# Two expert slots fetched as quarter rows and turned on VectorE instead of on TensorE

## The chip, the cores and the metric

The kernel runs on one core of a Trainium2 chip. The metric is device time in microseconds (us) for one execution. Three executions of the kernel before took 553.5, 553.92 and 554.93 us; their median is 553.92 us. A further execution was profiled, and took 553.22 us.

## The reference

For 8 batches of 8 heads, 576 positions and 64 dimensions, an attention through 32 memory columns, and behind it a mixture of 8 experts in which every token goes to one expert:

```
a = softmax(phi, axis=positions)                 # 32 memory columns a head
k_m, v_m = a^T k, a^T v                          # 32 x 64 a head
x = softmax(q k_m^T / 8) v_m                     # 4608 tokens x 512
e = argmax(x @ w_gate)                           # each token's expert, 8 of them
h = relu(x @ w1[e])                              # 512 -> 1024
out = softmax(x @ w_gate)[e] * sigmoid(x @ w_output_gate)[e] * (h @ w2[e])
```

All tensors are float32.

## The kernel before

The program has two overlapping parts. The attention runs for the first 110 us or so and writes its result x, with the gate factor of each token, as rows of 576 floats into the DRAM tensor `xs` (four groups of 144: 128 columns of x and 16 that hold the gate). The experts' work is a stream of *slots*. A slot is one expert and two or three blocks of 128 tokens which chose it. The tokens are not known beforehand: the kernel counts and ranks them on the chip while the attention runs (`rank`, `route_early`, `route_late`) and makes lists of row numbers with small matmuls (`table`). There are three lists: "a" serves slots 0 and 1, "b" serves slots 2, 3 and 4, and "l", which needs the whole attention, serves all later slots. In this data 14 slots run, 10 of three blocks and 4 of two.

A slot of three blocks goes through these steps. GpSimd gathers its rows from `xs` by indirect DMA into `xg` (`gather`, L538 and L532). The rows are turned so that the 512 columns of x lie on partitions, in four chunks (`turn_x`, chunk number c), and each chunk is split into a high part `xh` (a cast by ScalarE, L1091) and a low part `xl` (the rest, by VectorE, L1092). The *first half* of the slot on TensorE is 96 matmuls (L1241) that read the chunks in order 0, 1, 2, 3 for each of 8 output groups: per chunk one matmul with `xh`, one with `xl`, one with `xh` again. ScalarE (L1245) and VectorE (L1246) take their result out of PSUM. The *second half* is 72 matmuls (L1278) in 12 steps of 6; the results `y` are scaled by ScalarE (L1213) and scattered to the output by GpSimd (L1214), three DMAs a slot. The weights come as tiles `w` of 512 KB on SyncE's queue, each split into high and low part `whl` by ScalarE (L577) and VectorE (L591). After the attention has ended ten `whl` tiles are kept, so their splitting runs ahead of the matmuls.

Rows are turned in one of two ways. A *whole* slot is gathered with one DMA a block, three in all, and each chunk is turned by three TensorE transposes against the identity (L1089) into PSUM. A *quartered* slot is gathered with four DMAs a block, twelve in all, from an index list `idx_q` that puts row quarters so that VectorE's 32 x 32 block transpose (L1073) finishes the turn in SBUF. It also needs four small ScalarE copies (L1066) that gather the gate factors, and its `w` tiles are read from a copy with rows in another order. In the kernel before slots 0 to 4 are whole, and all later ones quartered.

The order of instructions on each engine is that in which the Python code emits them, and each engine works in order. While a slot's second half is emitted, `nxt(c)` emits the turn of the next slot's chunk c at steps 1, 4, 6, 9 and 10 (`TURN`). A whole slot uses the first four of these: transposes, `xh` and `xl` of chunk c together. A quartered slot uses all five: at c it emits VectorE's transpose of chunk c, and `xh` and `xl` of chunk c - 1. Behind every step `hook()` emits a few instructions of the routing that is still to be done (`route_late` up to the list "l"), which are mostly small VectorE operations between L346 and L272. `xg` has three buffers, so that a slot's gather can be emitted while the slot two before it runs.

Of the kernel before, what the change touches and what calls it, by code (L numbers as in the profile page):

```python
# [8 lines left out]
F32 = mybir.dt.float32  # L9
F32R = mybir.dt.float32r  # L10
BF16 = mybir.dt.bfloat16
I32 = mybir.dt.int32
# [5 lines left out]
P = 128  # L18
B, H, S, D, M = 8, 8, 576, 64, 32
NTOK, DM, E, F = 4608, 512, 8, 1024  # L20
# [8 lines left out]
NPS = (2, 3)  # L29
NPT, NPP, NSS = 5, 4, 22  # L30
NPE = sum(NPS)
NB3, NB2 = 3 * NPT, 2 * NPP
NBL = NB3 + NB2 + NSS
# [20 lines left out]
LATE = {"lg": 8, "w": 2, "ct": 8, "pe": 3, "dve": 2}  # L54
# [1 line left out]
PUMP = (2, 1)  # L56
TURN = {3: (1, 4, 6, 9, 10), 2: (0, 1, 2, 3, 4)}
LAST = 1
WHOLE = tuple(range(NPE))
XQ = 144  # L60
XROW = 4 * XQ

# [5 lines left out]
def attention_moe(tc, phiT, kv, qT, wgo, wall, out):  # L68
    nc = tc.nc
    V, A, G, T = nc.vector, nc.scalar, nc.gpsimd, nc.tensor  # L70

    with contextlib.ExitStack() as ctx:
        cp = ctx.enter_context(tc.tile_pool(name="cp", bufs=1))
# [4 lines left out]
        ident = cp.tile([P, P], F32, name="ident")  # L78
# [15 lines left out]
        idx = {}  # L94
        for nm, n in (("a", 3 * NPS[0]), ("b", 3 * NPS[1]), ("l", NBL)):
            idx[nm] = (cp.tile([P, n], I32, name="idx_g" + nm), cp.tile([P, n], I32, name="idx_o" + nm),
                       cp.tile([P, 4, n], I32, name="idx_q" + nm) if nm == "l" else None)
        slot = cp.tile([P, NSLOT + 1], I32, name="slot")
        ctx.enter_context(tc.manual_schedule())
        ohcs = [cp.tile([P, E], BF16, name=f"ohc{i}") for i in range(NBP)]  # L100
# [2 lines left out]
        rt = ctx.enter_context(tc.tile_pool(name="rt", bufs=1))  # L103
# [107 lines left out]
        def table(nm, q, nch, nblk):  # L211

            while nm == "l" and "rl" not in env:
                yield
            bw = (env["rl"] if nm == "l" else rt).tile([P, nch, 2, nblk], BF16, name="bw" + nm)
            w = min(nch, 9 * NBL // nblk // 9 * 9)
            for c in range(0, nch, w):
                b3 = [P, w, nblk]
                eq = rt.tile([P, 9 * NBL], BF16, name="eq")
                eq = eq[:, 0:w * nblk].rearrange("p (c b) -> p c b", c=w)  # L220
                V.tensor_tensor(eq, iota_blk[:, 0:nblk].unsqueeze(1).to_broadcast(b3),
                                q[:, c:c + w].unsqueeze(2).to_broadcast(b3), ALU.is_equal)
                yield
                for i in range(2):
                    V.tensor_tensor(bw[:, c:c + w, i], eq,
                                    tok_hl[:, i, c:c + w].unsqueeze(2).to_broadcast(b3), ALU.mult)
                yield
            yield
            yield from take_pr()
            yield from hold(LATE["pe"])  # L230
            pi = ps_r.tile([P, 2, NBL], F32, name="pr")
            for c in range(nch):
                T.matmul(pi[:, :, 0:nblk], Aw[:, c], bw[:, c], start=(c == 0), stop=(c == nch - 1))
            yield
            yield from hold(LATE["dve"])
            hl = rt.tile([P, 2, NBL], BF16, name="hl_i")
            iv = rt.tile([P, NBL], F32, name="iv")
            i2 = rt.tile([P, NBL], F32, name="i2")
            ivv, i2v, hlv = iv[:, 0:nblk], i2[:, 0:nblk], hl[:, :, 0:nblk]
            V.tensor_copy(hlv, pi[:, :, 0:nblk])  # L240
            yield
            V.scalar_tensor_tensor(ivv, hlv[:, 0], 64.0, hlv[:, 1], ALU.mult, ALU.add)
            if nm != "l":
                taken.clear()
            yield
            ig, io, iq = idx[nm]
            V.tensor_scalar(ig[:], ivv, 1.0, 0.0, ALU.subtract, ALU.max)
            V.tensor_scalar(i2v, ivv, 0.0, 100000.0, ALU.is_equal, ALU.mult)
            yield
            V.scalar_tensor_tensor(io[:], ivv, -1.0, i2v, ALU.add, ALU.add)  # L250
            if nm != "l":
                return
            for z in order:
                if z["nm"] == nm and not z["quart"]:
                    z["listed"] = True

            rep = env["rep"]
            pq = ps_r.tile([P, 4, 2, NBL], F32, name="pr")
            for b in range(4):
                T.matmul(pq[:, b, :, 0:nblk], rep[:, b], hlv, start=True, stop=True)  # L260
            yield
            yield from hold(LATE["dve"])
            t4 = env["rl"].tile([P, 4, NBL], F32, name="iq")
            t4v = t4[:, :, 0:nblk]
            V.tensor_copy(t4v, pq[:, :, 1, 0:nblk])
            yield
            V.scalar_tensor_tensor(t4v, pq[:, :, 0, 0:nblk], 64.0, t4v, ALU.mult, ALU.add)
            taken.clear()
            yield
            V.tensor_scalar(t4v, t4v, 1.0, 0.0, ALU.subtract, ALU.max)  # L270
            yield
            V.tensor_scalar(iq[:], t4v, 4.0, quad[:, 0:1], ALU.mult, ALU.add)  # L272
# [6 lines left out]
        def route_early(k):  # L279
# [48 lines left out]
            V.tensor_tensor(t1, t1, t3, ALU.mult)  # L328
            yield
            yield from table(nm, t1, nch, 3 * n)  # L330
            for z in order[s0:s0 + n]:
                z["listed"] = True
            if k == 0:
                gathers(0)
# [121 lines left out]
        env = {}  # L456
        clock = [0]

        taken = []

        def take_pr():

            while taken:
                yield
            taken.append(1)

        def hold(n):

            if "open" not in env:
                return  # L470
            end = clock[0] + n
            while clock[0] < end:
                yield

        def force():
            clock[0] += 1
            (rou if rou.gens else late if late.gens else att).step()
# [25 lines left out]
        for s in range(NSLOT):  # L503
            nb = 3 if s < NPE + NPT else 2 if s < NPE + NPT + NPP else 1
            if s < NPE:
                k = s >= NPS[0]
                nm, q0, rows = "ab"[k], 3 * (s - NPS[0] * k), (k + 2) * NCH * P
            else:
                j = s - NPE
                q0 = 3 * j if nb == 3 else NB3 + 2 * (j - NPT) if nb == 2 else NB3 + NB2 + j - NPT - NPP  # L510
                nm, rows = "l", NTOK
            slots.append({"s": s, "nb": nb, "q0": q0, "idx": idx[nm], "rows": rows,
                          "nm": nm, "quart": s not in WHOLE,
                          "known": False, "listed": False})
# [6 lines left out]
        def quarters(z, k):  # L521

            return 2 if (z["nb"], k) == (2, 1) else 4

        def gather(z):
            z["xg"] = xgs.tile()
            for k in range(z["nb"]):
                q = z["q0"] + k
                if z["quart"]:
                    rows = 4 * z["rows"]  # L530
                    for b in range(quarters(z, k)):
                        G.indirect_dma_start(  # L532
                            out=z["xg"][:, k, XQ * b:XQ * b + XQ], out_offset=None,
                            in_=xs[0:z["rows"]].rearrange("t (a q) -> (t a) q", a=4),
                            in_offset=bass.IndirectOffsetOnAxis(ap=z["idx"][2][:, b, q:q + 1], axis=0),
                            bounds_check=rows - 1, oob_is_err=False)
                    continue
                G.indirect_dma_start(  # L538
                    out=z["xg"][:, k], out_offset=None, in_=xs[0:z["rows"]],
                    in_offset=bass.IndirectOffsetOnAxis(ap=z["idx"][0][:, q:q + 1], axis=0),  # L540
                    bounds_check=z["rows"] - 1, oob_is_err=False)

        def known(*zs):
            for z in zs:
                z["known"] = True
# [64 lines left out]
        gat = [0, NPE + NPT + NPP]  # L610

        def gathers(i, must=0):

            while gat[0] < min(gat[1], i + xgs.size):
                z = order[gat[0]]
                if not z["listed"]:
                    if gat[0] >= must:
                        break
                    force()
                    continue  # L620
                gather(z)
                gat[0] += 1

        pa = ctx.enter_context(contextlib.ExitStack())
# [731 lines left out]
        def run(st):  # L1356
# [8 lines left out]
            def hook():  # L1365
                gathers(i)
                clock[0] += not att.gens
                att.step(HOOK[0])
                (rou if rou.gens else late).step(HOOK[1])

            for i in range(lo, hi):
                gathers(i, i + 1)
                if i == lo:
                    for c in range(5):
                        turn_x(order[i], c)

                def nxt(c):
                    if i + 1 < hi:
                        gathers(i, i + 2)
                        turn_x(order[i + 1], c)  # L1380

                if order[i]["nb"] > 1:
                    several(i, st, nxt, hook)
                else:
                    single(i, st, nxt)
                if "hs" not in env and (i == LAST or not att.gens):
                    settle()
# [6 lines left out]
        n = NPE + NPT + NPP  # L1394
# [52 lines left out]
```

## Time and profile before

| | |
|---|---|
| median of three executions | 553.92 us |
| the profiled execution | 553.22 us |
| its span in the trace | 551.5 us |
| TensorE matmuls busy | 507.9 us, 92% of the span |
| VectorE busy | 354.1 us, 64% |
| ScalarE busy | 288.0 us, 52% |
| GpSimd busy | 231.8 us, 42% |

Span and time of the profiled execution lie 1.7 us apart, which is launch and end. Busy shares are means over the span; matmuls are pipelined, so what a matmul costs is read from the distance of starts, not from its own duration. PE is TensorE, PEld its weight load, DVE VectorE, ACT ScalarE, POOL GpSimd, SP SyncE. Slot 0 starts at 119 us and slot 13 ends at 542 us.

### The profile page before, as it was taken

What the parts mean: (1) busy time and instruction counts of PE and PEld (TensorE: products, weight loads), DVE (VectorE), ACT (ScalarE), POOL (GpSimd) and SP (SyncE); (2) the same over time, 40 slices, a digit from 0 to 9 for tenths busy, and PEclk for the clock granted to TensorE, in tenths of its full rate; (3) what the DMA queues carried; (4) which work ended last, traced back from release to release, by engine and by line L of the source; (5) the groups of instructions that cost most, each with busy time, mean ns of one, the idle gap of its engine ahead of it and who ended that gap; (6) DMA issues with size and microseconds to landing.
All of it is one profiled execution on the core that took longest, in us unless ns stands there. A gap on an engine that the chain in (4) does not pass through costs nothing. (4 is left out here: it accounts for less than half of the span.)

```text
span 551.5 us, 10575 instructions
## 1 busy us (share of the span) xinstructions
PE 507.9 (92%) x3859; PEld 439.1 (80%) x3859; DVE 354.1 (64%) x779; ACT 288.0 (52%) x536; POOL 231.8 (42%) x254
## 2 busy tenths in 40 slices
PE   3788767689999999999999999999999999999993
PEld 2555545469789889898898989898999899888982
DVE  4376687877866659997454564954786387629310
ACT  3467465545535455553444545854785386548310
POOL 2244374860444134510467472655447363821101
PEclk9969799979999999999999999999999999999997
DMA  8999999995567756973466574876686577743001
GB/s 306 419 391 386 408 356 372 302 413 170 152 185 219 248 162 226 315 201 117 149 183 204 173 239 129 247 217 217 176 259 188 189 236 245 220 151 98 30 21 43
DMA packets 41998, 123.54 MB, mean 224 GB/s; under 512 B 10256, under 2 KB 10320, under 8 KB 41552
## 3 DMA queue, kind: packets, MB, share of 16 engines
q1 hardware_dynamic: 35136, 102.71, 56.5%
q0 software_dynamic: 6800, 20.06, 10.2%
q8 instruction: 32, 0.52, 0.4%
q14 instruction: 30, 0.25, 0.2%
HBM read 102.40 MB, written 20.35 MB: 223 GB/s over the span
## 5 line engine op out<-in xcount | busy, mean ns | idle before, releaser
L1278 PE MATMUL bps<-whl,hh 128*128 128x512 f32 x640 | 192.4, 393 | 0.0
L1241 PE MATMUL bps<-xh,whl 128*128 128x384 f32 x640 | 165.8, 336 | 0.0
L591 DVE TENSOR_TENSOR whl<-w,whl 128x1024 fp32r<-128x1024 f32 x112 | 138.2, 1239 | 10.9 <-ACT whl L577 10.8
L1278 PEld LDWEIGHTS bps<-whl,hh 128*128 128x128 f32 x640 | 119.9, 188 | 24.3 <-issue 0.2
L577 ACT CAST whl<-w 128x1024 fp32r<-128x1024 f32 x112 | 116.5, 1045 | 21.2 <-PE bps L1278 16.5
L1241 PEld LDWEIGHTS bps<-xh,whl 128*128 128x128 f32 x640 | 115.8, 188 | 1.1 <-ACT hh L1245 0.4
L532 POOL DMA_INDIRECT xg<-xs,idx_ql x84 | 97.3, 1158 | 25.6 <-issue 23.5
L1241 PE MATMUL bps<-xl,whl 128*128 128x384 f32 x320 | 107.0, 334 | 0.0
L1278 PE MATMUL bps<-whl,hl 128*128 128x512 f32 x240 | 93.7, 390 | 0.0
L1246 DVE SCALAR_TENSOR_TENSOR hl<-bps,hh 128x384 fp32r<-128x384 f32 x80 | 44.0, 554 | 60.3 <-ACT hh L1245 60.3
L1245 ACT ACTIVATE hh<-bps 128x384 fp32r<-128x384 f32 x80 | 38.9, 492 | 76.2 <-PE bps L1241 76.1
L1214 POOL DMA_INDIRECT out<-y,idx_ol x23 | 25.2, 1095 | 110.6 <-ACT y L1213 54.3
L1241 PEld LDWEIGHTS bps<-xl,whl 128*128 128x128 f32 x320 | 60.1, 188 | 0.3
L1278 PEld LDWEIGHTS bps<-whl,hl 128*128 128x128 f32 x240 | 45.1, 188 | 8.5
L1236 PE MATMUL bps<-xh,whl 128*128 128x384 f32 x128 | 37.7, 338 | 0.0
L872 POOL TENSOR_TENSOR ea<-ea,mx 128x512 f32<-128x512 f32 (+1 forms) x20 | 19.2, 960 | 43.3 <-DVE mx L870 39.0
L1237 PE MATMUL bps<-xh,whl 128*128 128x256 f32 x128 | 35.7, 279 | 0.0
L1213 ACT ACTIVATE y<-bps,gx 128x512 f32<-128x512 f32 x19 | 13.1, 687 | 40.0 <-PE bps L1278 33.4
L905 ACT COPY xo<-bpd 128x576 f32<-128x576 f32 x36 | 22.2, 641 | 21.4 <-PE bpd L903 9.7
L903 PE MATMUL bpd<-ve_b,aT 64*128 64x144 f32 (+1 forms) x320 | 28.6, 331 | 3.4 <-DVE ea L866 3.2
L1214 POOL DMA_INDIRECT out<-y,idx_ob x9 | 10.1, 1119 | 49.8 <-ACT y L1213 37.8
L988 POOL TENSOR_SCALAR Aw<-iota_row,row 128x128 bf16<-128x128 bf16 x36 | 26.0, 738 | 8.9 <-DVE row L978 8.9
(267 smaller groups left out, 588.2 us busy)
## 6 DMA issues: line engine op xcount, KB each, us to landing
w<-wall SPq DMA_DIRECT2D x112, 512.0 KB, 4.4
kvt<-kv SPq DMA_DIRECT2D x32, 512.0 KB, 8.1
xs<-xo SPq DMA_DIRECT2D x16, 576.0 KB, 7.4
qt<-qT SPq DMA_DIRECT2D x16, 512.0 KB, 8.5
ph<-phiT SPq DMA_DIRECT2D x3, 1152.0 KB, 11.7
kv<-kv SPq DMA_DIRECT2D x4, 512.0 KB, 8.5
xg<-xs,idx_ql POOLq DMA_INDIRECT x84, 4.5
ph<-phiT SPq DMA_DIRECT2D x4, 288.0 KB, 3.2
```

What stands on the lines that cost most here:

```text
L532: G.indirect_dma_start(out=z["xg"][:, k, XQ * b:XQ * b + XQ], out_offset=None, in_=xs[0:z["rows"]].rearrange("t (a q) -> (t a) q", a=4), i ...
L577: A.copy(hl[:, 0], w[:])
L591: V.tensor_tensor(hl[:, 1], w[:], hl[:, 0].bitcast(F32), ALU.subtract)
L903: T.matmul(px[to:to + n, r, sl], z["aT"][h, o:o + n], ves[2 * bp + b][h, g], start=True, stop=True)
L988: (G if AWP else V).tensor_scalar(Aw[:, bp * NCH + c], iota_row[:], row[:, c:c + 1], None, ALU.is_equal)
L1214: G.indirect_dma_start(out=out, out_offset=bass.IndirectOffsetOnAxis(ap=z["idx"][1][0:n, z["q0"] + k:z["q0"] + k + 1], axis=0), in_=y[0:n] ...
L1236: T.matmul(pb, w[:, 0, o:o + P], x[0][:, cc], start=(cc == 0), stop=False)
L1237: T.matmul(pb[:, 0:256], w[:, 1, o:o + P], x[0][:, cc, 0:256], start=False, stop=(cc == 3))
L1241: T.matmul(pb, w[:, b, o:o + P], x[a][:, cc, 0:n_], start=(n == 0), stop=(n == 11))
L1245: A.activation(h_[:, j], pb, AF.Relu)
L1246: V.scalar_tensor_tensor(l_[:, j], pb, 0.0, h_[:, j].bitcast(F32), ALU.max, ALU.subtract)
L1278: T.matmul(py[k], a, w[:, b, DM * f:DM * f + DM], start=(u == 4 and f == 0 and n == 0), stop=(u == 7 and f == 1 and n == len(ps) - 1))
```

## The change

Slots 3 and 4 become quartered. For that the list "b" also gets an index list of row quarters, `idx_qb`. The late list's is made with a tile `rep` of repeated identity slices in bfloat16, which does not exist yet when list "b" is made; list "b" uses sixteen matmuls of 128 x 32 identity slices on a float32 copy `hlf` of the list instead, into four 32-partition strips. The gather of slots 3 and 4 is emitted one DMA a hook. For all lists the quarter matmuls now first take the shared PSUM buffer (`take_pr`) and wait three hooks (`hold`), which moves those of list "l" too.

```
-WHOLE = tuple(range(NPE))
+WHOLE = (0, 1, 2)
...
-                       cp.tile([P, 4, n], I32, name="idx_q" + nm) if nm == "l" else None)
+                       cp.tile([P, 4, n], I32, name="idx_q" + nm) if nm != "a" else None)
...
+            if nm == "b":
+                hlf = rt.tile([P, 2, 3 * NPS[1]], F32, name="hlf", bufs=1)
+                A.copy(hlf[:], pi[:, :, 0:nblk])
...
-            if nm != "l":
-                taken.clear()
+            taken.clear()
...
-            if nm != "l":
+            if nm == "a":
                 return
...
-            rep = env["rep"]
+            yield from take_pr()
+            yield from hold(LATE["pe"])
             pq = ps_r.tile([P, 4, 2, NBL], F32, name="pr")
             for b in range(4):
-                T.matmul(pq[:, b, :, 0:nblk], rep[:, b], hlv, start=True, stop=True)
+                if nm == "l":
+                    T.matmul(pq[:, b, :, 0:nblk], env["rep"][:, b], hlv, start=True, stop=True)
+                else:
+                    for a in range(4):
+                        T.matmul(pq[32 * a:32 * a + 32, b, :, 0:nblk], ident[:, 32 * b:32 * b + 32], hlf[:],
+                                 start=True, stop=True)
...
-            t4 = env["rl"].tile([P, 4, NBL], F32, name="iq")
+            if nm == "l":
+                t4 = env["rl"].tile([P, 4, NBL], F32, name="iq")
+            else:
+                t4 = rt.tile([P, NSS, E], F32, name="cle")
...
                             bounds_check=rows - 1, oob_is_err=False)
+                        yield
                     continue
...
+            yield True
...
-                gather(z)
+                z.setdefault("gen", gather(z))
+                slow = z["nm"] == "b" and gat[0] >= must
+                while not next(z["gen"]):
+                    if slow:
+                        return
                 gat[0] += 1
```

Two places show how instructions move. The first is VectorE at the end of slot 2's second half, where slot 3's chunks are turned among the small operations of `route_late`. Before, from the `xl` of chunk 2 to just behind that of chunk 3:

```order
L1092 TENSOR_TENSOR xl<-bps,xh 128x384
L419 TENSOR_TENSOR cse<-cse 128x44
L421 TENSOR_TENSOR cse<-cse,kk 128x44
L423 TENSOR_TENSOR cse<-cse 128x22
L425 TENSOR_TENSOR slot<-cse 128x22
L203 TENSOR_TENSOR tm<-ohg,tb 128x288 x2
L591 TENSOR_TENSOR whl<-w,whl 128x1024
...
L430 TENSOR_TENSOR q_3276<-q_3276,jg 128x36
L431 TENSOR_TENSOR q_3279<-q_3279,jg 128x36
L1092 TENSOR_TENSOR xl<-bps,xh 128x384
L433 TENSOR_SCALAR ov<-q_3276,os 128x36
L435 TENSOR_TENSOR q_3276<-q_3276,ov 128x36
```

In the change (its line numbers are 12 to 18 higher: L1091 is the block transpose, L1110 is `xl`, L605 the low part of the weights), from the transpose of chunk 2 to the `xl` of chunk 3:

```order
L1091 STREAM_TRANSPOSE xt<-xg 128x384
L1110 TENSOR_TENSOR xl<-xt,xh 128x384
...
L203 TENSOR_TENSOR tm<-ohg,tb 128x288 x2
L605 TENSOR_TENSOR whl<-w,whl 128x1024
...
L442 TENSOR_TENSOR q_3352<-q_3352,jg 128x36
L443 TENSOR_TENSOR q_3355<-q_3355,jg 128x36
L1091 STREAM_TRANSPOSE xt<-xg 128x384
L1110 TENSOR_TENSOR xl<-xt,xh 128x384
L445 TENSOR_SCALAR ov<-q_3352,os 128x36
L447 TENSOR_TENSOR q_3352<-q_3352,ov 128x36
L1110 TENSOR_TENSOR xl<-xt,xh 128x384
L449 TENSOR_TENSOR q_3355<-q_3355,q_3352 128x36
```

The `xl` of chunk 2 now stands where that of chunk 3 stood, behind the transpose of chunk 3; the `xl` of chunk 3 stands one step later, behind two routing operations.

The second place is GpSimd from slot 1's second half on (`idx_gb` is list "b" by whole rows, `idx_qb` by quarters, `idx_ql` the late list by quarters, `out` the scatter of results). Before:

```order
L538 DMA xg<-xs,idx_gb 128x576 x6
L932 TENSOR_TENSOR w__2712<-lg,lm 128x72
L1214 DMA out<-y,idx_oa 4608x512 x3
L538 DMA xg<-xs,idx_gb 128x576 x3
L988 TENSOR_SCALAR Aw<-iota_row,row 128x128 x9
L1214 DMA out<-y,idx_ob 4608x512 x4
L532 DMA xg<-xs,idx_ql 128x144 x12
L1214 DMA out<-y,idx_ob 4608x512 x2
L532 DMA xg<-xs,idx_ql 128x144 x6
```

In the change:

```order
L551 DMA xg<-xs,idx_gb 128x576 x3
L544 DMA xg<-xs,idx_qb 128x144 x5
L950 TENSOR_TENSOR w__2743<-lg,lm 128x72
L544 DMA xg<-xs,idx_qb 128x144 x7
L1232 DMA out<-y,idx_oa 4608x512 x3
L544 DMA xg<-xs,idx_qb 128x144 x8
L1006 TENSOR_SCALAR Aw<-iota_row,row 128x128 x6
L544 DMA xg<-xs,idx_qb 128x144
L1006 TENSOR_SCALAR Aw<-iota_row,row 128x128 x3
L544 DMA xg<-xs,idx_qb 128x144 x3
L1232 DMA out<-y,idx_ob 4608x512 x6
L544 DMA xg<-xs,idx_ql 128x144 x18
```

Slots 3 and 4 take 24 gathers instead of 6, and the twelve gathers of slot 5 (the first of `idx_ql`) now stand behind all three scatters of slot 3, where they stood behind its first.

## Rows read from the trace of the kernel before

**Rows 1.** The page: busy us and share of the span by engine; and busy tenths of TensorE and VectorE in 40 slices of 13.8 us.

```profile
PE 507.9 (92%) x3859; PEld 439.1 (80%) x3859; DVE 354.1 (64%) x779; ACT 288.0 (52%) x536; POOL 231.8 (42%) x254
PE   3788767689999999999999999999999999999993
DVE  4376687877866659997454564954786387629310
```

**Rows 2.** Busy time of each engine in two stretches: the end of slot 2's first half with its second half and the start of slot 3, then most of slot 3. Behind the counts stand the granted clock, the DMA share and GB/s.

```profile
209.00:242.00 33.00, 33.00 (x173) 29.82 (x172) 32.49 (x98) 19.00 (x27) 13.43 (x13) 1.00 0.75 246
243.00:270.00 27.00, 27.00 (x168) 23.48 (x167) 19.69 (x36) 10.88 (x17) 1.11 (x2) 1.00 0.47 143
```

**Rows 3.** TensorE in order of time (start, duration): the first row of slot 2's second half, the matmul before one group of slot 3's transposes and the two starts behind it, the start of slot 3's first half and of its second, and the starts of slot 4's second half and of slot 5.

```profile
216.24 0.39 PE L1278 MATMUL bps<-whl,hh 128*128 128x512 f32 x1
...
218.77 0.39 PE L1278 MATMUL bps<-whl,hh 128*128 128x512 f32 x1
219.01 0.49 PE L1089 MATMUL bps<-ident,xg 128*128 128x128 f32 x3
219.25 0.48 PE L1278 MATMUL bps<-whl,hh 128*128 128x512 f32 x1
219.57 0.39 PE L1278 MATMUL bps<-whl,hl 128*128 128x512 f32 x1
...
234.07 0.33 PE L1241 MATMUL bps<-xh,whl 128*128 128x384 f32 x1
...
250.73 0.39 PE L1278 MATMUL bps<-whl,hh 128*128 128x512 f32 x1
...
287.12 0.39 PE L1278 MATMUL bps<-whl,hh 128*128 128x512 f32 x1
...
303.48 0.33 PE L1241 MATMUL bps<-xh,whl 128*128 128x384 f32 x1
```

**Rows 4.** TensorE in order of time during the attention: two runs of sixteen small float32 matmuls with 32 weight columns, each with the row that follows it.

```profile
16.34 0.71 PE L765 MATMUL pk<-kv,a 128*32 128x128 f32 x16
16.98 0.28 PE L771 MATMUL pk<-zero 1*128 1x256 bf16 x1
...
19.42 0.32 PE L805 MATMUL bpa<-wg,vT_b 64*32 64x16 f32 x16
19.66 0.66 PE L736 MATMUL bpa<-ident,ph 128*128 128x128 f32 x4
```

**Rows 5.** VectorE in order of time: the last row before the stretch of rows 2 with an idle time ahead of it (in brackets, with what ended it), slot 3's four `xl`, and the rows behind the fourth.

```profile
208.64 0.56 DVE L1246 SCALAR_TENSOR_TENSOR hl<-bps,hh 128x384 fp32r<-128x384 f32 x1 [1.24 <-ACT hh L1245]
...
222.07 0.55 DVE L1092 TENSOR_TENSOR xl<-bps,xh 128x384 fp32r<-128x384 f32 x1
...
226.70 0.55 DVE L1092 TENSOR_TENSOR xl<-bps,xh 128x384 fp32r<-128x384 f32 x1
...
230.50 0.55 DVE L1092 TENSOR_TENSOR xl<-bps,xh 128x384 fp32r<-128x384 f32 x1
...
234.58 0.55 DVE L1092 TENSOR_TENSOR xl<-bps,xh 128x384 fp32r<-128x384 f32 x1
235.05 0.23 DVE L433 TENSOR_SCALAR ov<-q,os 128x36 f32<-128x36 f32 x1
...
235.54 0.20 DVE L437 TENSOR_TENSOR q<-q,q 128x36 f32<-128x36 f32 x1
```

**Rows 6.** VectorE in order of time while slot 5, a quartered one, is turned: two block transposes and an `xl`, each with the row that follows it, and the `xl` of chunk 3.

```profile
289.90 0.58 DVE L1073 STREAM_TRANSPOSE xt<-xg 128x384 f32<-128x384 f32 x1 [0.36 <-DMA out<-y,idx_ob]
290.40 1.18 DVE L591 TENSOR_TENSOR whl<-w,whl 128x1024 fp32r<-128x1024 f32 x1
291.51 0.57 DVE L1073 STREAM_TRANSPOSE xt<-xg 128x384 f32<-128x384 f32 x1
292.00 0.52 DVE L1092 TENSOR_TENSOR xl<-xt,xh 128x384 fp32r<-128x384 f32 x1
292.43 1.22 DVE L591 TENSOR_TENSOR whl<-w,whl 128x1024 fp32r<-128x1024 f32 x1
...
303.49 0.56 DVE L1092 TENSOR_TENSOR xl<-xt,xh 128x384 fp32r<-128x384 f32 x1 [0.79 <-ACT xh L1091]
```

**Rows 7.** GpSimd in order of time: slot 2's third scatter, the first and last gather of slot 5, and the first gather behind slot 4's third scatter; and ScalarE's row that first needed the last of slot 5's gathers.

```profile
240.53 1.15 POOL L1214 DMA_INDIRECT out<-y,idx_ob  x1 [3.35 <-ACT whl L577]
...
269.86 1.47 POOL L532 DMA_INDIRECT xg<-xs,idx_ql  x1 [0.30 <-issue]
...
284.99 1.25 POOL L532 DMA_INDIRECT xg<-xs,idx_ql  x1 [0.30 <-issue]
...
312.54 1.04 POOL L532 DMA_INDIRECT xg<-xs,idx_ql  x1 [0.30 <-issue]
...
289.59 0.19 ACT L1066 COPY gx<-xg 32x3 f32<-32x3 f32 x1 [0.32 <-DMA xg<-xs,idx_ql]
```

**Rows 8.** Windows as in rows 2 at two pauses of TensorE during the attention and behind the first of them; and one form of matmul in order of time in the second of these windows and in the expert stage.

```profile
78.00:81.30 3.30, 0.04 (x1) 0.05 (x1) 2.25 (x6) 1.32 (x5) 3.30 (x6) 1.00 1.04 350
81.50:84.70 3.20, 3.20 (x43) 2.53 (x49) 0.82 (x4) 1.97 (x5) 1.94 (x3) 0.50 1.04 334
88.30:91.50 3.20, 1.51 (x44) 0.92 (x36) 2.99 (x12) 0.91 (x3) 1.63 (x4) 1.00 1.03 409
...
81.92 2.29 PE L903 MATMUL bpd<-ve_b,aT 64*128 64x144 f32 x16
...
170.71 1.25 PE L903 MATMUL bpd<-ve_b,aT 64*128 64x144 f32 x16
```

More of the change, by code (lines that the diff above doesn't have):

```diff
@@ L255, in table @@
                     z["listed"] = True
-            rep = env["rep"]
+            yield from take_pr()
+            yield from hold(LATE["pe"])
             pq = ps_r.tile([P, 4, 2, NBL], F32, name="pr")
             for b in range(4):
-                T.matmul(pq[:, b, :, 0:nblk], rep[:, b], hlv, start=True, stop=True)
+                if nm == "l":
[4 more added lines that the diff above has]
+                                 start=True, stop=True)
             yield
             yield from hold(LATE["dve"])
-            t4 = env["rl"].tile([P, 4, NBL], F32, name="iq")
+            if nm == "l":
+                t4 = env["rl"].tile([P, 4, NBL], F32, name="iq")
+            else:
+                t4 = rt.tile([P, NSS, E], F32, name="cle")
+                t4 = t4[:].rearrange("p a b -> p (a b)")[:, 0:4 * nblk].rearrange("p (a b) -> p a b", a=4)
             t4v = t4[:, :, 0:nblk]
```

## The prediction

> **What bounds the kernel now.** I read the page first, then windows, then TensorE and the engines that feed it in order of time. Over the span TensorE is busy 92% and VectorE 64% [rows 1]; from slice 9 on, where the slots run, TensorE stands at 9 in every slice. So the time is set by TensorE's work behind 119 us and by each pause in it. The windows show the second thing: from 209 to 242 us VectorE too is busy, 32.49 of 33.00 us, and from 243 to 270 only 19.69 of 27.00 [rows 2]. In order of time VectorE last waits for something at 208.64 us [rows 5]; behind that it works through a queue that is already there. There the routing of `route_late`, the weights that fill the ten `whl` tiles and slot 2's own results come together. The reader is to see that TensorE does not wait for this yet: slot 3 starts at 234.07 us, right behind slot 2 [rows 3], while the last thing it needs, the `xl` of its chunk 3, runs from 234.58 to 235.13 us [rows 5]. A first half of 96 matmuls takes 16.66 us (234.07 to 250.73) [rows 3], 0.174 us each, and that `xl` is read by its eleventh matmul, at 234.07 + 10 x 0.174 = 235.81. The slack is 0.7 us.
>
> **What it removes.** Slots 3 and 4 lose 24 TensorE transposes, in eight groups of three. A second half without transposes takes 303.48 - 287.12 = 16.36 us, slot 2's, with four groups, takes 234.07 - 216.24 = 17.83 [rows 3]. From 218.77 to 219.57 there are two stream matmuls (2 x 16.36 / 72 = 0.45 us) and one group, 0.35 us. Four groups are thus 1.4 to 1.47 us, and two slots give back 2.8 us.
>
> **What it adds on TensorE.** Sixteen small float32 matmuls with 32 weight columns and 18 data columns. The trace has no such form; sixteen with 16 columns and half the rows take 19.66 - 19.42 = 0.24 us, sixteen with 128 columns 16.98 - 16.34 = 0.64 us [rows 4]. I take 0.4 us. They stand in slot 1 and shift everything behind alike.
>
> **What it moves to VectorE.** Eight block transposes of 0.50 us (289.90 to 290.40) [rows 6]; in slot 4 they lie in a stretch with idle time [rows 2], and cost nothing as long as that lasts. The four index operations and ScalarE's copy `hlf` fall into slot 1, before the queue builds; the eight copies of gate factors on ScalarE, 0.2 us each [rows 7], lie beside casts. In slot 3 the transposes enter the full queue, and the order matters more than their length. Up to chunk 2's `xl` in the change, four transposes are new and one `xl` fewer stands ahead (0.43 us, 292.00 to 292.43) [rows 6]. Chunk 2's `xl` stands where chunk 3's did, so it starts at 234.58 + 4 x 0.50 - 0.43 = 236.15 and ends 0.52 later, at 236.67. TensorE ends slot 2 at 216.24 + 16.36 = 232.60 and needs that `xl` for its eighth matmul, at 233.82. It waits 2.85 us. Behind chunk 2's `xl` come two routing operations, 235.54 - 235.05 = 0.49 us [rows 5], then chunk 3's `xl`: it ends at 236.15 + 0.43 + 0.49 + 0.52 = 237.59, three matmuls after the restart would be 237.19. Another 0.4, together 3.25 us. Bounds: if the earlier transposes found gaps, only chunk 3's own would count and the wait would be 234.58 + 0.50 + 0.52 - 233.82 = 1.8 us; if ScalarE's cast of chunk 3, which stands between two VectorE operations, came last, another 0.5 us, 3.75 in all. I take 3.25, since rows 2 leave half a microsecond of gaps in 33. Who waits behind it: slot 3's results and `y` by as much; of weights ten tiles are ahead.
>
> **What it moves on GpSimd.** The gathers of slots 3 and 4 have over 20 us to spare each: twelve at about 1.4 us are 17 us and start where three started. Slot 5 is different. Its twelve gathers now follow slot 3's third scatter. Slot 2's third scatter starts 6.5 us behind its slot's end (240.53 - 234.07) and lasts 1.15, so a gather could start at +7.9; behind slot 4's it starts at +9.1 (312.54 - 303.48) [rows 3, 7]. I take +8.5 behind slot 3's end. From slot 5's first gather to the first use of its last data were 289.59 - 269.86 = 19.7 us [rows 7]: data at +28.2. From there ScalarE and VectorE need four transposes, three weight splits of 1.11 (290.40 to 291.51) between them [rows 6], four `xl` and ScalarE's first cast, about 7.7 us to chunk 3's `xl`: +35.9. TensorE, through slot 4 without transposes, needs it at 16.66 + 16.36 + 1.74 = +34.8. A wait of 1.1 us, with +7.9 one of 0.5, with +9.1 one of 1.7; with the spare of the 269.86 start none. I take 1.1.
>
> **The clock.** A pause can cost more than itself. Behind 78.00 to 81.30 us, in which TensorE did 0.04 us of work, its granted clock was 0.50, the 1.2 GHz level, for 81.50 to 84.70; behind 88.30 to 91.50, with 1.51 us of work, no fall is seen [rows 8]. At the lower level sixteen matmuls of one form took 2.29 us, at 2.4 GHz 1.25 [rows 8], so 3.2 us at the lower level lose 3.2 x (1 - 1.25 / 2.29) = 1.45 us. A pause of 3.25 us resembles the first case more. If part of the low stretch lies on the pause itself it costs less; between 0 and 1.45 I take 1.0.
>
> **The sum.** -2.8 + 0.4 + 3.25 + 1.1 + 1.0 = +2.95 us, on 553.22 us: 556.2. The profiled execution lies 0.7 us under the median and under all three timed ones, so the same sum on the median gives 556.9. I predict 556.7 us.
>
> **Two rules against the trace.** The rows give 0.12 us of TensorE's time per transpose. The Trainium skill ("VectorE: DVE Perf Modes", The three transpose paths) gives a 128 x 128 transpose 390 ns on TensorE in bfloat16 and 311 ns on VectorE, in blocks; by that figure 24 of them would be an estimated 9.4 us on TensorE, and no run here shows one alone. By the rows' starts it is a third of that. The shares of the whole span say that TensorE is the engine to relieve and VectorE the one with room [rows 1]. The Trainium skill ("Perfetto Trace Analysis", Identifying the Most-Contended Engine) says to optimize the engine with the highest occupancy, and by that alone the change would bring 2.4 us; it adds that the most contended engine can change over time, and with that rows 2 agree.
>
> **The rivals.**
> - *The gain stands* (0.13). VectorE's transposes hide, and the time is 553.9 - 2.8 + 0.4 = 551.5 us. It needs chunk 2's `xl` to end by 233.82, that is 2.85 us earlier in the queue than I put it, and slot 5's data by +27. For it: slot 5 itself is turned this way without a wait at 303.48 [rows 3], with its last `xl` at 303.49 [rows 6]. Against it: VectorE had idle time there and has none here. The same side holds if a transpose frees its whole duration instead of its place in the stream: 8 x 0.49 = 3.9 us [rows 3], and nothing waits: 553.9 - 3.9 + 0.4 = 550.4. By the same rows the two second halves differ by 1.47 us only, so I give it 0.02.
> - *Part of the wait* (0.15). VectorE's queue has gaps that the transposes fill, the wait is the lower bound of 1.8 us, the clock stays, slot 5 is in time: 553.9 - 2.8 + 0.4 + 1.8 = 553.3, no change.
> - *The waits without the clock* (0.22): 553.9 - 2.8 + 0.4 + 3.25 + 0.3 to 1.1 = 555.0 to 555.9, on both sides of the mark.
> - *My forecast* (0.42): 555.6 to 558.
> - *More* (0.06): the clock falls twice, or slot 5 waits 1.7 us too: 558.5 and up.
>
> **Numbers.** About 0.3%, 1.7 us, is what can be told from no change. Faster holds the first rival, 0.15. Same holds the second and half of the third, 0.27. Slower 0.58. The range leaves out the best and worst cases: 552.6 to 558.6; the forecast's own is 555.6 to 558.
>
> **What would show it.** Right: TensorE's second halves of slots 2 and 3 shorter by 1.4 us each, a pause of 2 to 4 us inside slot 3's first ten matmuls released by `xl`, VectorE without idle time up to it, a granted clock under 1.00 close behind it, slot 5's first transpose some 8 us later than before relative to its slot. Wrong: slot 3's first half at 16.7 us, or slot 4's or 5's start later than named; a small matmul run above 0.7 us; or idle time on VectorE between 210 and 235 us, which would mean that its queue is not what I read.

## The result, and the profile after

The changed kernel takes 557.82 us (median of 11 executions), the kernel before 553.5 us beside it (11 executions). The ratio is 1.0085, with a 95% interval from 1.0066 to 1.0104: slower by 0.85%, clear of the noise, 1.1 us above the forecast of 556.7 and inside its range. The profiled execution took 557.64 us with a span of 555.9 us, 4.4 us more than before.

The page, by engine and in slices of 13.9 us:

```profile
PE 511.4 (92%) x3867; PEld 440.0 (79%) x3867; DVE 356.8 (64%) x791; ACT 289.1 (52%) x545; POOL 260.3 (47%) x272
PE   3788887889999999889999999999999999999992
DVE  4374979677867649989454374954786397639210
```

Beside [rows 1] the shares say nothing, but TensorE's two slices of 8 behind slice 15 are new: they hold the start of slot 3. TensorE in order of time (start, duration; in brackets the idle time ahead of the row and what ended it): the small matmuls in slot 1, the starts of the halves of slots 2 to 4, slot 5's start, the last matmul.

```profile
174.19 0.45 PE L267 MATMUL pr<-hlf,ident 128*32 128x18 f32 x32
...
216.82 0.39 PE L1296 MATMUL bps<-whl,hh 128*128 128x512 f32 x1
...
233.19 0.33 PE L1259 MATMUL bps<-xh,whl 128*128 128x384 f32 x1
...
234.07 0.52 PE L1259 MATMUL bps<-xh,whl 128*128 128x384 f32 x2
237.69 0.69 PE L1259 MATMUL bps<-xl,whl 128*128 128x384 f32 x1 [3.10 <-DVE xl L1110]
238.18 0.84 PE L1259 MATMUL bps<-xh,whl 128*128 128x384 f32 x2
238.82 0.58 PE L1259 MATMUL bps<-xl,whl 128*128 128x384 f32 x1
...
240.76 0.34 PE L1259 MATMUL bps<-xl,whl 128*128 128x384 f32 x1
...
254.64 0.39 PE L1296 MATMUL bps<-whl,hh 128*128 128x512 f32 x1
...
272.88 0.33 PE L1259 MATMUL bps<-xh,whl 128*128 128x384 f32 x1
...
289.55 0.39 PE L1296 MATMUL bps<-whl,hh 128*128 128x512 f32 x1
...
305.91 0.33 PE L1259 MATMUL bps<-xh,whl 128*128 128x384 f32 x1
...
544.93 0.39 PE L1296 MATMUL bps<-whl,hh 128*128 128x512 f32 x1
```

Slot 2's second half lasts 233.19 - 216.82 = 16.37 us, where it lasted 17.83 [rows 3]; slot 3's second half 272.88 - 254.64 = 18.24, where it was 287.12 - 16.66 - 250.73 = 19.73 [rows 3]. Between them slot 3's first half lasts 254.64 - 233.19 = 21.45 us in place of 16.66 [rows 3]: the two gains are 1.46 and 1.49 us, the loss 4.79. Windows around that loss, as in [rows 2]:

```profile
233.00:237.30 4.30, 1.59 (x9) 1.22 (x7) 4.20 (x14) 0.85 (x3) 3.39 (x4) 1.00 0.70 217
237.30:240.60 3.30, 2.90 (x9) 2.70 (x10) 3.23 (x9) 0.45 (x1) 0.66 (x1) 0.50 0.60 231
240.80:255.00 14.20, 14.20 (x83) 14.16 (x82) 12.09 (x26) 7.82 (x13) 1.99 (x2) 1.00 0.48 148
```

First TensorE waits while VectorE is busy 4.20 of 4.30 us; then TensorE works at a granted clock of 0.50, its 1.2 GHz level, and the nine matmuls from 237.69 on take 240.76 - 237.69 = 3.07 us, where nine take 9 x 0.174 = 1.57 us at the rate of a first half without a pause; then all is as before. VectorE in that stretch, from the first turn of slot 3 on:

```profile
222.80 0.58 DVE L1091 STREAM_TRANSPOSE xt<-xg 128x384 f32<-128x384 f32 x1 [0.19 <-DMA xg<-xs,idx_qb]
...
227.97 0.59 DVE L1110 TENSOR_TENSOR xl<-xt,xh 128x384 fp32r<-128x384 f32 x1
...
232.58 0.51 DVE L1110 TENSOR_TENSOR xl<-xt,xh 128x384 fp32r<-128x384 f32 x1
...
236.63 0.57 DVE L1091 STREAM_TRANSPOSE xt<-xg 128x384 f32<-128x384 f32 x1
237.12 0.52 DVE L1110 TENSOR_TENSOR xl<-xt,xh 128x384 fp32r<-128x384 f32 x1
...
238.12 0.55 DVE L1110 TENSOR_TENSOR xl<-xt,xh 128x384 fp32r<-128x384 f32 x1
...
242.83 0.56 DVE L1264 SCALAR_TENSOR_TENSOR hl<-bps,hh 128x384 fp32r<-128x384 f32 x1 [1.97 <-ACT hh L1263]
```

The bracket at 222.80 is the only idle time that the rows mark on VectorE from 209 to 240 us; chunk 2's `xl` starts at 237.12, and 237.69 is where TensorE goes on. The second place where a wait was forecast is slot 5: GpSimd's first and last gather for it, and VectorE with its data.

```profile
280.86 0.98 POOL L1232 DMA_INDIRECT out<-y,idx_ob  x1 [4.91 <-issue]
282.14 1.04 POOL L544 DMA_INDIRECT xg<-xs,idx_ql  x1 [0.30 <-issue]
...
297.04 1.00 POOL L544 DMA_INDIRECT xg<-xs,idx_ql  x1 [0.31 <-issue]
...
299.69 0.58 DVE L1091 STREAM_TRANSPOSE xt<-xg 128x384 f32<-128x384 f32 x1 [7.73 <-DMA xg<-xs,idx_ql]
...
305.91 1.21 DVE L1110 TENSOR_TENSOR xl<-xt,xh 128x384 fp32r<-128x384 f32 x2
```

The gathers start 282.14 - 272.88 = 9.3 us behind slot 3's end, as [rows 7] would have it for a slot behind a scatter. The last `xl` ends at 305.91 + 1.21 = 307.1, and TensorE, which starts slot 5 at 305.91, wants it 1.74 us later: no wait.

The last matmul comes 2.73 us later than before (542.20 there). The other 1.7 us lie behind it: from there to the end of the span it is 11.0 us, before 9.3. The chain of work that ended last, after (start, duration, what):

```profile
540.92 0.98 DMA out<-y,idx_ol
541.90 4.39 issue
546.29 0.50 POOLq L1414
546.80 0.68 POOL out L1232
```

The chain ends in the last scatter; what comes behind it is not in the chain. In the trace's records of GpSimd two long instructions stand there, a semaphore step and a drain, called the last drain here: 0.795 and 2.530 us before, 1.155 and 4.000 us after, together 1.83 us more. Two short drains behind them take 0.107 and 0.045 us in both kernels.

### The profile page after: what moved, and what is told of

Same layout as the page of the kernel before. It is cut to its first block, busy times and chain, and to the rows that moved or that the text cites. A ratio compares the mean times of both kernels' runs of the same rounds, so it can differ in the third digit from the quotient of the medians.

```text
span 555.9 us, 10650 instructions
## 1 busy us (share of the span) xinstructions
PE 511.4 (92%) x3867; PEld 440.0 (79%) x3867; DVE 356.8 (64%) x791; ACT 289.1 (52%) x545; POOL 260.3 (47%) x272
## 5 line engine op out<-in xcount | busy, mean ns | idle before, releaser
L1296 PE MATMUL bps<-whl,hh 128*128 128x512 f32 x640 | 190.2, 392 | 0.0
L605 DVE TENSOR_TENSOR whl<-w,whl 128x1024 fp32r<-128x1024 f32 x112 | 137.5, 1233 | 13.3 <-ACT whl L591 13.3
L544 POOL DMA_INDIRECT xg<-xs,idx_ql x84 | 102.2, 1216 | 25.6 <-issue 23.5
L1231 ACT ACTIVATE y<-bps,gx 128x512 f32<-128x512 f32 x25 | 17.2, 688 | 55.7 <-PE bps L1296 38.5
L544 POOL DMA_INDIRECT xg<-xs,idx_qb x24 | 28.1, 1170 | 10.9 <-issue 6.3
```

The lines of the kernel that those rows point to most:

```text
L544: G.indirect_dma_start(out=z["xg"][:, k, XQ * b:XQ * b + XQ], out_offset=None, in_=xs[0:z["rows"]].rearrange("t (a q) -> (t a) q", a=4), i ...
L605: V.tensor_tensor(hl[:, 1], w[:], hl[:, 0].bitcast(F32), ALU.subtract)
L1296: T.matmul(py[k], a, w[:, b, DM * f:DM * f + DM], start=(u == 4 and f == 0 and n == 0), stop=(u == 7 and f == 1 and n == len(ps) - 1))
```

## The experiments

My theory (A) was: VectorE's full queue in slot 2's second half makes slot 3's `xl` late, and the clock falls behind the pause. The rivals were that the index work holds slot 3 up (B), that slot 4's gathers on GpSimd do (D), or that slot 3's rows land too late (E). On the longer end (C): the last drain grows with the number of indirect transfers.

**One slot at a time.** The first kernel keeps slot 3 whole, the second slot 4.

```
-WHOLE = (0, 1, 2)
+WHOLE = (0, 1, 2, 3)      # q4only
+WHOLE = (0, 1, 2, 4)      # q3only
```

> Only slot 4 is fetched as quarters; slot 3 is fetched whole and turned on TensorE as before. The index work (small matmuls, the list of quarters) stays. Theory A (VectorE's full queue in slot 2's second half makes slot 3's low copies late): no pause, slot 3's first half 16.7 us at clock 1.0, as in the kernel before; slot 2's second half back at 17.8 us. Sum on the 553.2 us of before: 0.6 for the small matmuls in slot 1, 1.5 off slot 3's second half, 0.3 to 0.9 at the end of the program: 552.5 to 553.5 us. Theory B (the index work in the lists is what holds slot 3 up): slot 3's first half is still near 21 us, and the time is 556.5 to 558 us. Theory C (the end of the program grows with the number of GpSimd's indirect transfers): 9 more transfers, so from the last matmul to the end 10.1 us, between 9.3 and 11.0; if the longer end of the changed kernel was chance, 9.3 or any other value without order.

> Only slot 3 is fetched as quarters; slot 4 is whole and turned on TensorE in slot 3's second half. Theory A: slot 3's first half stays at 21 to 21.5 us with a pause near 3.1 us and a low clock behind it; slot 3's second half is 19.7 us as before; the time is 0.6 + 4.8 - 1.5 = 3.9 us over the 553.2 of before and 0.3 to 0.9 more at the end: 557.4 to 558.1 us. Theory D (slot 4's quarters, which GpSimd issues among its other work in slot 2, delay slot 3's data or its index work): without them slot 3's first half falls towards 16.7 us and the time to 552.5 to 554 us. Theory C: from the last matmul to the end 10.1 us.

Slot 4 alone: 553.68 us, 0.9995 of the kernel before (0.9973 to 1.0016). Slot 3 alone: 558.82 us, 1.0087 (1.0055 to 1.0119). The windows over slot 3's start and behind it, slot 4 alone and then slot 3 alone, and for the latter TensorE's wait between 200 and 330 us (total, times, longest):

```profile
233.00:241.00 8.00, 8.00 (x47) 7.80 (x46) 7.80 (x21) 4.51 (x7) 2.22 (x3) 1.00 0.69 221
241.00:270.00 29.00, 29.00 (x175) 25.74 (x175) 22.10 (x45) 12.20 (x21) 1.77 (x2) 1.00 0.50 147
```

```profile
233.00:241.00 8.00, 5.09 (x21) 4.29 (x20) 7.83 (x24) 3.63 (x6) 1.74 (x2) 0.86 0.68 238
241.00:270.00 29.00, 29.00 (x179) 26.48 (x179) 22.00 (x43) 11.48 (x17) 0.97 (x1) 0.98 0.45 130
PE bps L1259 <- DVE xl L1110: 2.8, 1, 2.8
```

With slot 4 alone TensorE is busy 8.00 of 8.00 us there, and slot 3's first half lasts 16.67 us although the index work stays: B falls. With slot 3 alone the pause is 2.8 us and the half lasts 21.59 us, without slot 4's gathers: D falls. The time of this kernel lies 0.7 us above the upper end of what was named for it. The whole loss belongs to slot 3's turns, and slot 4 by itself is neither gain nor loss.

**Slot 3's turns queued earlier on VectorE.**

```
-                if step in TURN[nb]:
-                    nxt(TURN[nb].index(step))
+                turn = (1, 3, 4, 5, 6) if i == 2 else TURN[nb]
+                if step in turn:
+                    nxt(turn.index(step))
```

> The changed kernel with slot 3's turns and splits put earlier in slot 2's second half: steps 1, 3, 4, 5, 6 in place of 1, 4, 6, 9, 10 of its 12 steps, so that slot 3's low copies of chunks 2 and 3 are queued on VectorE 4 steps (5.4 us) earlier, ahead of list pieces and two or three weight splits of 1.2 us. Theory A: they are computed 3 to 5 us earlier, at 232 to 235 in place of 237.1 and 238.1 us; the pause shrinks from 3.1 us to 0 to 0.6 and the granted clock stays 1.0; slot 3's first half is 16.7 to 17.5 us, and the time 552.5 to 554.5 us. Theory E (slot 3's rows themselves land too late, since the first turn already waited 0.19 us for its rows): the turns wait for the rows, the pause stays at 2.5 us or more, and the time stays at 557 us or more.

553.46 us, 0.9997 (0.9969 to 1.0025). VectorE's `xl` of chunks 1 to 3, and the start of slot 3's first half:

```profile
230.82 0.52 DVE L1110 TENSOR_TENSOR xl<-xt,xh 128x384 fp32r<-128x384 f32 x1
...
232.19 0.51 DVE L1110 TENSOR_TENSOR xl<-xt,xh 128x384 fp32r<-128x384 f32 x1
235.62 0.55 DVE L1110 TENSOR_TENSOR xl<-xt,xh 128x384 fp32r<-128x384 f32 x1
...
235.02 0.33 PE L1259 MATMUL bps<-xh,whl 128*128 128x384 f32 x1
```

Chunk 2's `xl` now ends 2.3 us ahead of the start (232.70 against 235.02), though this profile's slots begin 1.9 us later. Slot 3's first half lasts 16.67 us at a clock of 1.00. E falls, and A stands: the order of the queue was the cause. Counted from slot 0's first matmul to the last one TensorE takes 421.3 us, 423.2 in the kernel before and 426.0 in the changed one. So on TensorE the change is worth 1.9 us in this profile once its rows are turned in time, and the end of the program, 11.3 us here against 9.3, takes it back. Of the 2.95 us that the transposes took, 0.6 go into the small matmuls and 0.5 into slot 3's second half, 18.75 us here against 18.24, in which the late list's matmuls now wait for VectorE.

**The end of the program.** The first kernel adds 18 gathers of 64 bytes a row to the kernel before; the second 46 of 32 rows; the third takes 45 away.

```
+                if z["s"] in (3, 4):
+                    for r in range(3):
+                        G.indirect_dma_start(out=spare[:, r], out_offset=None, ...)     # tail18
+                if z["nm"] == "l":
+                    for r in range(2):
+                        G.indirect_dma_start(out=spare[:, r], out_offset=None, ...)     # tail46: index [0:32]
-WHOLE = tuple(range(NPE))
+WHOLE = tuple(range(NPE + NPT))                                                         # lwhole
```

> The kernel before with 18 more indirect transfers on GpSimd: ahead of each of the six gathers of slots 3 and 4 three gathers of 64 bytes a row into a tile that nothing reads. TensorE's work is that of before, last matmul at 542.2 us. Theory C (the end of the program grows with the number of indirect transfers): from the last matmul to the end 11.0 us in place of 9.3, GpSimd's last drain near 4.0 us in place of 2.5, the time 554.5 to 555.3 us. If the longer end comes from something else (the size of what is in flight, or chance): 9.3 us, last drain 2.5 us, and the time 552.8 to 553.6 us.

> The kernel before with 46 more gathers of 32 rows (the others fetch 128), two ahead of each block of the slots from 5 on, into a tile that nothing reads; they may delay those slots' rows, so only the end of the program is read. GpSimd's last drain took 2.530, 3.265 and 4.000 us after 137, 146 and 155 indirect transfers, 0.0817 us for each. If it is paid by the transfer: 2.530 + 46 x 0.0817 = 6.29 us, and the semaphore step before it 0.795 + 46 x 0.020 = 1.72 us. If it is paid by the row: a quarter of that, 3.47 and 1.03 us. If it were a count that starts again after some number of transfers: less than 2.5 us.

> The kernel before with the five three-block slots from 5 on fetched whole as well and turned on TensorE: 45 indirect transfers fewer, 92 in all. On the line of 0.0817 us each the last drain would be 2.530 - 45 x 0.0817, below zero: so it is either near nothing (the line starts at about 106 transfers), or the line has another form below 137. TensorE pays 1.5 us for each of the five slots, 7.4 us, and the end of the program gives back up to 2.5 + 0.8 = 3.3 us: 556 to 558.5 us. If the end is shortened by more than 3.3 us, the waits ahead of the drain belong to it too.

From the records of GpSimd in each trace (the last two rows are the next experiment's, profiled beside each other on one chip):

```
kernel                        indirect    slot 0 to     last matmul   semaphore   last
                              transfers   last matmul   to the end    step        drain
before                        137         423.2         9.3           0.795       2.530
changed                       155         426.0         11.0          1.155       4.000
slot 4 alone (q4only)         146         422.3         10.3          0.975       3.265
slot 3 alone (q3only)         146         427.6         10.3          0.975       3.265
earlier turns (early)         155         421.3         11.3          1.155       4.000
18 more (tail18)              155         426.9         10.7          1.155       4.000
46 more of 32 rows (tail46)   183         454.8         12.4          1.435       5.138
45 fewer (lwhole)             92          430.4         15.3          2.028       7.593
earlier turns, drained        155         420.9         6.7           0.248       0.306
before, drained               137         423.8         7.2           0.248       0.306
```

From 137 to 155 it is a straight line, to the last digit: (3.265 - 2.530) / 9 = 0.0817 us a transfer in the drain and 0.020 in the semaphore step, whichever slot the transfers belong to. The 18 tiny gathers give exactly the changed kernel's 4.000 us, so the longer end is neither chance nor the rows' size. Their kernel took 559.3 us, 1.0104 (1.0062 to 1.0147), more than I expected: slots 1 and 3 became 3.6 us longer, and TensorE's longest new wait in them, 1.7 us, is for the routing, of which GpSimd does a part. The two other kernels took 587.69 and 568.72 us beside 554.72, one execution each. The former's slots waited much, as its 454.8 us show. The latter's did not: its 430.4 us are 7.2 above the kernel before, the transposes of five slots as named (7.4). But it was forecast at 556 to 558.5 us with a shorter end, and its end is 6.0 us longer; the rest, 2.2 us, lies ahead of slot 0, which starts at 121.17 us. The line does not go on below: with 92 transfers the drain is the longest of all. 92 x 0.0817 + 0.08 = 7.6 is what a line from nearly zero gives, and on the same line 2.530, 3.265 and 4.000 us are 30, 39 and 48 transfers, each 107 fewer than were made. So the count seems to start again once, somewhere between 92 and 137; this is argued from the one kernel below 137 and not shown. The 46 small ones gave 5.138 us, between the two prices that I had named; what a transfer of fewer rows counts stays open.

**A drain ahead of the end.** If the last drain pays for what has piled up, it can be paid where GpSimd is idle, between the halves of the last slot.

```
+            if 8 * i + 8 == st.hi:
+                G.drain()
             py = [bank([DM], "ps") for _ in range(nb)]
```

> The changed kernel with the earlier turns of slot 3, and one more drain on GpSimd between the two halves of the last slot, where GpSimd has nothing to do for some 17 us. If a drain works off what the indirect transfers before it have left behind, the middle one takes about 4 us and the last one only what the last three scatters leave, under 0.5 us; with the semaphore step's 0.02 us a transfer the end of the program shrinks from 11.0 to 7.5 us or less, and the time is 553.5 - 3.5 to 4.6: 549 to 550 us, faster than both kernels. If the last drain counts all transfers whatever was drained: last drain 4.0 us and the time stays at 553.5 us.

> The kernel before with the same one line, a drain on GpSimd between the halves of the last slot. If a drain works off what is left behind: the middle one takes about 2.5 us, the last one under 0.5, and the time falls by 2.1 to 2.9 us against the kernel before. Otherwise nothing moves. Beside the other run of this call it shows what the earlier turns and the quarters of slots 3 and 4 are worth when the end of the program no longer counts them: 1.4 to 1.9 us.

In both the last drain fell to 0.306 us, under the 0.5 that was named, and the semaphore step to 0.248. The middle drains took 4.89 and 3.97 us in the records, more than the 4 and 2.5 named. The kernel before became 553.31 us, 0.9959 (0.9931 to 0.9987). The one with earlier turns became 562.33, 1.0106 (1.0071 to 1.0141), against its expectation. TensorE's waits from 200 to 330 us in it:

```profile
PE pr L233 <- DVE bwl L225: 3.8, 2, 2.6
PE bps L1298 <- issue: 3.6, 2, 1.8
PE bps L1259 <- DVE xl L1110: 0.4, 1, 0.4
```

Slot 3's second half lasted 24.83 us there: the late list's matmuls (L233), which stand in TensorE's queue between the stream's, waited for VectorE. Slot 4's second half lasted 23.46, and in it a cast of a weight began after 3.34 us of idle time, most likely because the weight itself came late. In both halves the granted clock fell as well (0.67 over 260 to 270 us, 0.78 over 310 to 320). To part the drain from the chip, I ran both pairs again on one chip, with slot 4 alone and the drain as a fourth.

> The kernel of the earlier turns once more, on the same chip as the next three, since it stood at 553.5 us on one chip and, with one drain added, at 562.3 on another. If the drain itself costs: this one is again level with the kernel before (0.997 to 1.003) and the one with the drain 1.01. If the earlier turns leave the list of the last slots so late that small delays of a chip decide (in the profile of that run the list's matmuls waited 3.8 us for VectorE, and weights came late in slot 4): both move together, and the one with the drain is 3.5 to 4.6 us faster than this one.

> Earlier turns and drain, on the same chip as the one without the drain. If the drain is free where it stands: 3.5 to 4.6 us below that one, last drain 0.31 us again, from the last matmul to the end 7.0 us. If the drain costs elsewhere: above it by 4 to 9 us.

> Only slot 4 as quarters, with the drain. TensorE: 1.5 us off slot 3's second half, 0.6 for the small matmuls, VectorE's queue in slot 2 as in the kernel before; the end of the program 7.0 us in place of 10.3. Against the kernel before: 0.9 + 2.3 = 3.2 us less, 550.5 us on its 553.7, faster than both kernels; 0.9 us below the kernel before with the drain. If the drain costs elsewhere: level with the kernel before or slower.

> The kernel before with the drain, again, beside the three others: 2.1 to 2.9 us below the kernel before, as it was on the other chip (0.9959), and 0.9 us above the one that fetches slot 4 as quarters too.

Beside 553.75 us of the kernel before: earlier turns 553.41 us, 0.9993 (0.9964 to 1.0022); the same with the drain 549.58, 0.9878 (0.9831 to 0.9925); slot 4 alone with the drain 550.8, 0.9928 (0.9905 to 0.9951); the kernel before with the drain 550.63, 0.9917 (0.989 to 0.9944). GpSimd at the end of the earlier turns with the drain:

```profile
513.69 0.91 POOL L1232 DMA_INDIRECT out<-y,idx_ol  x1 [2.52 <-ACT hh L1263]
531.98 0.98 POOL L1232 DMA_INDIRECT out<-y,idx_ol  x1 [17.38 <-ACT y L1231]
```

The middle drain, 4.89 us from 513.46 on, ends 13.6 us before GpSimd's next scatter at 531.98, which waits for the last slot's first `y`. The scatter of 513.69 lies inside that record, so the 4.89 us are not the pile's alone; what else is in them stays open. So the drain is free where it stands, and its gain is 3.1 us in the kernel before and 3.8 us with earlier turns on this chip, 2.1 us in the kernel before on the other. The earlier turns are another matter: here the list's matmuls waited 0.5 us without the drain and not at all with it, on the other chip 3.8 us. Why VectorE, and most likely the weights, were late on that chip stays open, and the earlier turns without the drain were not run there; the kernel before took 555.43 us there, 1.7 us more than here. With the drain in both, the earlier turns should have stood 1.4 to 1.9 us below the kernel before: here they stand 1.05 us below it with overlapping intervals, on the other chip 9.0 us above it, so their worth is not settled. The safe version is the kernel before with the one drain, faster on both chips, by 0.4 and 0.8%; the 0.9 us by which slot 4's quarters should have beaten it were not seen in four executions each.

## Why the prediction was right, and where it was not

Direction and mechanism held. That the total came out as near as 4.4 us against 2.95 is partly luck: 1.1 us were named for a wait that did not come, and 1.7 us at the end of the program were not named at all.

- **Transposes removed.** 2.8 us named, 1.46 + 1.49 = 2.95 measured. The price came from the distance of starts in [rows 3], and it held for both slots.
- **Small matmuls.** 0.4 us named, between 0.24 and 0.64; slot 1's first half became 0.61 us longer (18.88 to 19.49). The range was misread: the sixteen new matmuls appear as 32 rows, and the two runs of sixteen rows in [rows 4] are likewise eight matmuls each (L765 and L805 each emit two groups of four). By those rows sixteen matmuls would be 0.48 to 1.28 us, and what was measured lies near the cheaper form.
- **The pause.** 3.25 us named, at the matmul that was named, released by the `xl` that was named. The row's 3.10 us count from the modelled end of the matmul before; by starts, as the prediction reckons, TensorE stood from 234.07 + 2 x 0.174 = 234.42 to 237.69, 3.27 us. That the sum fits so well is luck: the first wait was named 2.85 us and was 3.27, and the second, 0.4 us for chunk 3, did not come. Chunk 3's `xl` ends at 238.12 + 0.55 = 238.67, and at the lower clock TensorE reaches the matmul that reads it at 238.82. [rows 2] and the queue of [rows 5] were the right place to look: 32.49 of 33.00 us busy meant that a late entry moves everything behind it.
- **The clock.** 1.0 us named, between 0 and 1.45; 3.07 - 1.57 = 1.5 measured. With the 3.27 us of the pause that is 4.77 of the 4.79 us. [rows 8] were the right case, a pause of this size and a stretch at 1.2 GHz behind it, and the upper bound was near what came. The 1.0 was too low since it let a third of the low stretch fall on the pause: the windows put only 0.4 us of it there, from 237.3 on.
- **Slot 5.** 1.1 us named, nothing paid. The gathers started as late as I put it, even a little later (+9.3 for +8.5). The step that failed is the time from the first gather to the data: 19.7 us in [rows 7], but 299.69 - 282.14 = 17.6 here. The twelve gathers themselves start within 14.9 us here and 15.1 there; from the last of them to its data it was 289.59 - 284.99 = 4.6 us there and 299.69 - 297.04 = 2.65 here. I had taken the one distance in the trace for a fixed one; why it was shorter stays open.
- **The end of the program.** Nothing named, 1.7 us measured: the term that the sum lacked. The semaphore step and the last drain grew by 1.83 us, the stretch from the last matmul to them was 0.14 shorter. I had costed the 18 more indirect transfers on GpSimd as hidden, by the room ahead of slots 3 and 4, and had not looked at what GpSimd does behind its last scatter.
- 0.3 us in slot 7's first half (16.67 to 16.97) I did not follow up. The kernel with slot 3 alone has them too, those with slot 4 alone and with earlier turns do not; the cause stays open.

Of the rivals, the gain that stands is what the earlier turns show on TensorE: 1.9 us less than before without the pause, where I had named 2.4.

The Trainium skill ("Perfetto Trace Analysis", Optimization Strategy) says that the most contended engine can change over time. The windows of this case agree: VectorE, 64% busy over the span, was busy 32.49 of the 33.00 us in which slot 3's chunks were due [rows 2].

## What to carry to other kernels

Before work is moved to an engine with room, look at its queue in the stretch where the work must be done, and at the place in that queue: slot 3's four block transposes cost TensorE 4.8 us at one place in the queue, and up to four steps of TensorE earlier its first half kept its 16.67 us. Count what the change issues over the whole program, and look behind the last result too, where a drain may pay for all of it. A pause of TensorE of 3.3 us cost 1.5 us more in clock here.

## What the hardware showed that I had not expected

GpSimd's last drain is not a fixed cost: 0.306 to 7.593 us here. From 137 to 155 indirect transfers of 128 rows each one more costs 0.0817 us in it, and 0.020 us in the semaphore step ahead of it. A drain earlier in the program takes this away: 0.306 us were left, with 137, 146 and 155 transfers alike. More transfers are not always dearer: 92 left 7.593 us, 137 left 2.530. The Trainium skill ("VectorE: DVE Perf Modes", The DRAIN you can't avoid) calls the drains at a program's end boilerplate of some 12 ns on every engine; the other engines' here are near that, 7 to 17 ns, but GpSimd's long one is not, and the measurement decides.
